# First batch's second and last third: one operation for all three feature blocks

## The chip, the cores and the metric

The kernel runs on one core of one Trainium2 chip. The metric is the device time of one execution in microseconds (us), 441.68 in the median of three runs (441.19 to 444.34). The engines are named as in the profile: PE does matmuls (PEld loads their weights), DVE, ACT and POOL do elementwise work, SP issues the DMA transfers. Each engine works through its own queue in order.

## The reference, cut to what matters

For 4 batches, 768 positions and 384 features (8 heads of 48), a linear attention with a complex decay runs first, and its output y is the input of a mixture of 4 attention experts:

```
mag = sqrt(a_re^2 + a_im^2); scale = min(mag, 0.999) / (mag + 1e-6)
S[t] = (a[t] * scale) * S[t-1] + k[t] v[t]^T   (complex, per feature d)
y[t] = q[t] . Re S[t]
for each expert e: q, k, v = x @ wq[e], wk[e], wv[e]
  a = causal softmax(q k^T / 8);  ye = a @ v @ wo[e]
out = sum over the two experts with the highest gate logits of w * ye
```

## The kernel before, in words

Features lie on the 128 partitions in three feature blocks j = 0, 1, 2 (384 = 3 x 128), positions in the free dimension. The recurrence is done in chunks of 128 positions: `logs` and `angles` turn the decay into running sums of log magnitude and angle by scans, and q and k are multiplied by exp, sin and cos of them (`logs`, `sincos`, `products`). For one j this takes about a dozen ACT activations in two table sets (logarithm and exponential, sine and arctangent), three scans per third on DVE or one long one, and a dozen products and other two-operand operations on DVE or POOL. The real and imaginary parts of q and k then lie in tile `qk`; `regroup` sends them by DMA to tile `fm`, where a head's 96 rows stand together: ten transfers (DMA issues on SP) for one third of a batch, three, four and three of them for j = 0, 1, 2.

From `fm`, PE works on pairs of chunks: transposes (`pk`), scores (`psc`, masked by DVE into `pts`), states (`pu`; `wst` and `tst` on DVE or POOL), outputs (`yu`, split by ACT and DVE into the tile `x`), then the expert projections (`proj`: `pp`, `qka`; `vproj`: `pv`), row maxima (`maxpass`: `pm`, DVE) and, once all six chunks are through, `rowmax` (`mrow`), `score` (`pss`, exponentials `pe` on ACT), `av` (`po`), `norm` (`dn`, `r`, `ot`) and `wo` (`pw`, `ob`, the output transfer).

Batches 1 to 3 take a whole feature block of 768 positions in one operation. Batch 0 is worked out in three thirds of 256 positions, so that its first third reaches PE early: the loop over `c` and `j` in `record` calls each step for one third and one feature block.

What runs when is written out by hand in tables. ORDER lists all operations, and since each engine runs its own in that order, the list sets every queue. HOME moves an operation to another engine than its own. ROOMS gives each tile its buffer. FILL names operations of PE ahead of which so many fill matmuls are issued: 128x512 products of the constant `keep` into a result buffer that the operation overwrites.

Of the kernel before, what the change touches and what calls it, by code (L numbers as in the profile page):

```python
# [40 lines left out]
HOME = {39: 'vector',  # L41
 54: 'vector',
 62: 'vector',
 69: 'vector',
# [108 lines left out]
 1420: 'gpsimd',
 1426: 'gpsimd',
 1428: 'gpsimd',
 1448: 'gpsimd',
 1450: 'gpsimd',
 1455: 'gpsimd',
 1463: 'gpsimd',
# [31 lines left out]
 1775: 'vector',
 1782: 'vector',
 1784: 'vector',
 1836: 'gpsimd',
 1858: 'gpsimd',
 1860: 'gpsimd',
 1868: 'gpsimd',
 1876: 'gpsimd',
 1929: 'vector',
 1935: 'vector'}  # L200

FILL = {297: 138, 358: 14, 376: 1, 407: 3, 460: 15, 466: 4, 509: 3, 737: 6}

ROOMS = {'ab': [0, 1, 0, 1, 0, 1, 0, 1, 0, 0, 1, 0],
 'carry': [0, 1, 0, 3, 1, 2],
 'fm': [0, 1, 0, 0, 1, 0, 1, 0, 1, 0, 1, 0],
 'gcf': [0, 0, 0, 0],
 'gmx': [0, 0, 0, 0],
# [744 lines left out]
```

## Time and profile before

| | |
|---|---|
| median of three runs | 441.68 us |
| profiled execution | 442.14 us, of which the span is 440.1 us |
| PE busy | 409.8 us (93%), fill matmuls among it |
| DVE busy | 367.6 us (84%), 758 instructions |
| ACT busy | 290.2 us (66%), 485 instructions, 37 table loads of 1.28 us among them |
| POOL busy | 149.9 us (34%), 153 instructions |
| granted clock of PE | 0.996 over the span |

The span runs from the first to the last instruction. Busy time of PE holds the fill matmuls too, so its share does not tell how much of the span is the program's own work. Of the other engines the share is an average over stages: in the first 120 us they are nearly full, in the last 140 us they are not.

### The profile page before, as it was taken

How to read it: one execution, taken by the hardware profiler on the slowest of the kernel's cores; microseconds unless marked ns; L12 is line 12 of the kernel's file. 1: busy time of each engine (PE TensorE's matmuls, PEld its weight loads, DVE VectorE, ACT ScalarE, POOL GpSimd, SP SyncE). 2: the span in 40 equal slices, each digit the busy share in tenths (PEclk: the TensorE clock that was granted, in tenths of full speed). 3: DMA queues.
4: the chain of work that ended last, by engine and by line, in shares of the span. 5: the costliest groups of instructions: out<-in, count | busy, mean ns of one | idle time of the engine just before them, and what ended most of it. 6: DMA issues, size and time to landing. Idle time of an engine off the chain costs nothing.

```text
span 440.1 us, 9745 instructions
## 1 busy us (share of the span) xinstructions
PE 409.8 (93%) x3804; PEld 329.3 (75%) x3804; DVE 367.6 (84%) x758; ACT 290.2 (66%) x485; POOL 149.9 (34%) x153
## 2 busy tenths in 40 slices
PE   7998897878899998997999989999999999999996
PEld 3447686856568886886879878788888988888675
DVE  6999989989977999999886899999876436798563
ACT  6999979788852899875644899777733313113562
POOL 0005212414340333494723533562625032200620
PEclk9999999899999999999999999999999999999999
DMA  8752759352463851303873810353371600101002
GB/s 268 284 160 57 194 178 318 97 180 68 103 193 82 229 186 36 104 2 87 255 208 101 247 65 2 110 162 108 103 194 35 176 3 18 55 20 37 19 1 107
DMA packets 28173, 53.40 MB, mean 121 GB/s; under 512 B 3552, under 2 KB 8928, under 8 KB 28128
## 3 DMA queue, kind: packets, MB, share of 16 engines
q1 hardware_dynamic: 28128, 52.79, 41.0%
q8 instruction: 30, 0.49, 0.5%
q14 instruction: 15, 0.12, 0.1%
HBM read 26.74 MB, written 4.72 MB: 71 GB/s over the span
## 4 chain that ended last, share of the span: by engine, by line
PE 51%; DVE 21%; ACT 17%; issue 5%; DMA 3%; POOL 2%; SPq 1%; DVEq 0%; ACTq 0%; POOLq 0%
DVE qk L897 9%; PE pss L897 8%; PE pp L897 7%; PE po L897 6%; ACT qk L897 5%; PE yu L897 5%; PE psc L897 5%; PE pw L897 5%; ACT ab L897 5%; ACT L895 4%; PE pu L897 3%; PE pv L897 3%; DVE ab L897 3%; DVE junk L897 3%; PE dn L897 2%
## 5 line engine op out<-in xcount | busy, mean ns | idle before, releaser
L897 ACT ACTIVATE pe<-pss 128x1024 f32<-128x1024 f32 (+2 forms) x48 | 43.3, 916 | 23.3 <-PE pss L897 19.7
L897 PE MATMUL psc<-fm 96*128 96x128 f32 x384 | 53.0, 285 | 5.2 <-DVE pts L897 2.1
L897 POOL TENSOR_TENSOR pe<-pe 128x512 f32<-128x512 f32 (+2 forms) x31 | 39.4, 1272 | 47.8 <-DVE pe L897 23.9
L897 PEld LDWEIGHTS psc<-fm 96*128 96x128 f32 x384 | 47.1, 194 | 9.8 <-DVE pts L897 2.4
L897 ACT ACTIVATE ab<-ab 128x768 f32<-128x768 f32 (+1 forms) x72 | 45.8, 654 | 8.7 <-DVE ab L897 7.3
L897 ACT ACTIVATE qk<-qk 128x256 f32<-128x256 f32 (+3 forms) x84 | 45.6, 563 | 7.4 <-DVE qk L897 5.7
L897 POOL TENSOR_TENSOR qk<-qk,ab 128x768 f32<-128x768 f32 (+1 forms) x25 | 39.0, 1568 | 28.6 <-ACT ab L897 16.0
L895 ACT ACT_TABLE_LOAD x37 | 47.5, 1283 | 1.4 <-PEq L942 0.8
L897 PE MATMUL pp<-x,whi 128*128 128x256 f32 x288 | 47.2, 287 | 0.5 <-DVE pts L897 0.3
L897 PE MATMUL pss<-qka 64*128 64x256 f32 (+3 forms) x480 | 46.4, 304 | 1.1 <-ACT pe L897 1.1
L897 PE MATMUL po<-pe,v 128*64 128x256 f32 (+3 forms) x320 | 43.5, 395 | 0.0
L897 POOL TENSOR_TENSOR qk<-qk 128x768 f32<-128x768 f32 (+1 forms) x18 | 25.1, 1406 | 53.8 <-ACT qk L897 47.7
L897 PEld LDWEIGHTS pss<-qka 64*128 64x128 f32 x480 | 35.5, 185 | 10.4 <-issue 4.2
L897 PEld LDWEIGHTS pp<-x,whi 128*128 128x128 f32 x288 | 38.9, 188 | 3.6 <-issue 1.1
L897 POOL TENSOR_SCALAR_AFFINE_SELECT pe<-pe 128x256 f32<-128x256 f32 x48 | 22.0, 474 | 53.0 <-ACT pe L897 52.9
L897 DVE TENSOR_TENSOR pts<-psc,keep 128x512 f32<-128x512 f32 x48 | 32.5, 683 | 9.1 <-PE yu L897 4.8
L886 PEld LDWEIGHTS <-keep 128*128 128x128 bf16 x184 | 18.1, 101 | 24.9 <-issue 3.0
L886 PE MATMUL psc<-keep 128*128 128x512 bf16 x144 | 33.6, 397 | 2.6 <-DVE keep L897 2.6
L897 DVE CUSTOM_DVE_ANT_0 junk<-pm,negm 128x128 bf16<-128x128 f32 (+3 forms) x64 | 31.0, 485 | 2.0 <-PE pm L897 0.3
L897 PE MATMUL pw<-whi,ot 128*128 128x384 f32 x96 | 28.6, 351 | 3.4 <-DVE qka L897 2.5
L897 DVE TENSOR_TENSOR qk<-qk,ab 128x256 f32<-128x256 f32 (+1 forms) x47 | 30.9, 688 | 0.9 <-ACT qk L897 0.3
L897 PE MATMUL yu<-pts,vt 128*64 128x128 f32 x384 | 27.7, 283 | 4.0 <-DVE pts L897 4.0
(118 smaller groups left out, 907.7 us busy)
## 6 DMA issues: line engine op xcount, KB each, us to landing
fm<-qk SPq DMA_DIRECT2D x72, 192.8 KB, 3.7
qk<-in_ak_dram SPq DMA_DIRECT2D x12, 768.0 KB, 6.9
ab<-in_ak_dram SPq DMA_DIRECT2D x18, 384.0 KB, 4.5
...
```

What stands on the lines that cost most here:

```text
L886: nc.tensor.matmul(z, real(plan.busy), real(plan.busy)[:, None, :].to_broadcast([128, 4, 128]), start=True, stop=True)
L895: nc.scalar.preload_act_table_set(need)
L897: getattr(getattr(nc, engine), name)(*a, **k)
```

## The change: batch 0's thirds 1 and 2 for all feature blocks at once

In batch 0 the first third is still worked out feature block by feature block. For the second and the last third each step is now called once for the three blocks: operations on 128x256 become operations on 128x3x256. The scans over positions stay 256 long. For this the twelve tiles `qk` (one per batch and feature block, in three rooms) become one tile with a place for each feature block, which all batches use, and the three decay tiles of a third become one with the part before the feature block. ORDER, HOME, FILL and ROOMS are new throughout. ACT now has 435 instructions in its queue and had 487, DVE 727 and had 760, POOL 145 and had 158, SP 224 as before; PE has the same matmuls in a new order, with 164 fill matmuls where there were 184 (135 ahead of the first real one, where there were 138). The number of table loads is the same.

The diff without the tables ORDER, HOME and ROOMS (rows of their effect stand below it):

```diff
-FILL = {297: 138, 358: 14, 376: 1, 407: 3, 460: 15, 466: 4, 509: 3, 737: 6}
+FILL = {199: 3, 205: 1, 211: 135, 217: 3, 227: 11, 262: 3, 370: 7, 405: 1}
...
@@ -407,7 +387,9 @@
     def cst(shape, dtype, name):
         return p.tile(shape, dtype, name)
 
-    ab, early, qk, fm, vt, xk, qka, v2, lgs, mrow, mx, ot = ({} for _ in range(12))
+    ab, early, fm, vt, xk, qka, v2, lgs, mrow, mx, ot = ({} for _ in range(11))
+
+    qk = p.tile([128, 3, 2, NK, KW], F32, "qk")
 
     def load_decay(b, j, k0, k1, split):
         n = (k1 - k0) * C2
@@ -415,8 +397,8 @@
             t = ab[b, j, k0] = p.tile([128, 2, n], F32, "ab")
         else:
             if k0 not in early:
-                early[k0] = p.tile([128, 3, 2, n], F32, "ab")
-            t = ab[b, j, k0] = early[k0][:, j]
+                early[k0] = p.tile([128, 2, 3, n], F32, "ab")
+            t = early[k0][:, :, j]
         x = ak[b, j, :, :2 * S].rearrange("p (x c) -> p x c", x=2)[:, :, k0 * C2:k1 * C2]
         for i in range(2):
             if split:
@@ -425,9 +407,7 @@
                 p.dma(t, x)
 
     def load_qk(b, j, k0, k1):
-        if (b, j) not in qk:
-            qk[b, j] = p.tile([128, 2, NK, KW], F32, "qk")
-        p.dma(qk[b, j][:, 0, k0:k1, :2 * C2], ak[b, j, :, 2 * S:].rearrange("p (k x) -> p k x", k=NK)[:, k0:k1])
+        p.dma(qk[:, j, 0, k0:k1, :2 * C2], ak[b, j, :, 2 * S:].rearrange("p (k x) -> p k x", k=NK)[:, k0:k1])
 
     def load_v(b, k):
         vt[b, k] = p.tile([128, 2, H, HD], F32, "vt")
@@ -487,69 +467,84 @@
             p.copy(whi[:, s], t)
             p.tt(V, wlo[:, s], t, mid(whi[:, s]), OP.subtract)
 
-    def views(b, j, k0, k1):
-        t, u = ab[b, j, k0], qk[b, j]
-        A, Bi = (t[:, i] for i in range(2))
-        flat = [x.rearrange("p (k x) -> p k x", x=C2) for x in (A, Bi)]
-        Q, K, X, Y = (u[:, i, k0:k1, o:o + C2] for i in range(2) for o in (0, C2))
-        return A, Bi, *flat, Q, K, X, Y, u[:, :, k0:k1, 2 * C2:]
-
-    def logs(b, j, k0, k1):
-        A, Bi, Af, Bf, Q, K, X, Y, E = views(b, j, k0, k1)
-        p.act(X, Af, AF.Ln)
-        p.act(Af, X, AF.Exp, scale=-1.0)
+    def views(b, js, k0, k1):
+        if b:
+            j = js[0]
+            t = ab[b, j, k0].rearrange("p i (k x) -> p i k x", x=C2)
+            Q, K, X, Y = (qk[:, j, i, k0:k1, o:o + C2] for i in range(2) for o in (0, C2))
+        else:
+            s = slice(js[0], js[-1] + 1)
+            t = early[k0][:, :, s]
+            Q, K, X, Y = (qk[:, s, i, k0, o:o + C2] for i in range(2) for o in (0, C2))
+        return t[:, 0], t[:, 1], Q, K, X, Y
+
+    def logs(b, js, k0, k1):
+        A, Bi, Q, K, X, Y = views(b, js, k0, k1)
+        n = NK if b else len(js)
+        p.act(X, A, AF.Ln)
+        p.act(A, X, AF.Exp, scale=-1.0)
         p.mul(V, Bi, Bi, A)
         p.act(A, Bi, AF.Square)
-        p.act(Y, Af, AF.Ln, bias=1.0)
+        p.act(Y, A, AF.Ln, bias=1.0)
         p.stt(X, Y, 0.5, X, OP.mult, OP.add)
         p.act(Y, X, AF.Exp, scale=-1.0)
         p.act(Y, Y, AF.Ln, scale=1e-6, bias=1.0)
         p.stt(X, X, math.log(0.999), Y, OP.min, OP.subtract)
-        for k in range(k1 - k0):
+        for k in range(n):
             p.put(V, "tensor_tensor_scan", X[:, k], cmask, X[:, k], 0.0, op0=OP.mult, op1=OP.add)
         p.act(Y, X, AF.Exp)
-        p.copy(E.rearrange("p x k c -> p k x c"),
-               Y.rearrange("p k (c t) -> p k c t", t=C)[:, :, None, :, C - 1].to_broadcast([128, k1 - k0, 2, 2]))
+        ends = Y.rearrange("p k (c t) -> p k c t", t=C)[:, :, None, :, C - 1].to_broadcast([128, n, 2, 2])
+        if b:
+            p.copy(qk[:, js[0], :, k0:k1, 2 * C2:].rearrange("p x k c -> p k x c"), ends)
+        else:
+            p.copy(qk[:, js[0]:js[-1] + 1, :, k0, 2 * C2:], ends)
         p.mul(V, Q, Q, Y)
         p.act(X, X, AF.Exp, scale=-1.0)
         p.mul(V, K, K, X)
 
-    def atan(b, j, k0, k1):
-        A, Bi = views(b, j, k0, k1)[:2]
+    def atan(b, js, k0, k1):
+        Bi = views(b, js, k0, k1)[1]
         p.act(Bi, Bi, AF.Arctan)
 
-    def angles(b, j, k0, k1):
-        A, Bi, Af, Bf, Q, K, X, Y, E = views(b, j, k0, k1)
+    def angles(b, js, k0, k1):
+        A, Bi = views(b, js, k0, k1)[:2]
         n = (k1 - k0) * C2
-        p.put(V, "tensor_tensor_scan", A, ones.to_broadcast([128, n]), Bi, last.get((b, j), 0.0), op0=OP.mult, op1=OP.add)
-        if k1 < NK:
-            last[b, j] = p.tile([128, 1], F32, "carry")
-            p.put(V, "tensor_copy", last[b, j], A[:, n - 1:n])
+        if b:
+            flat = [x.rearrange("p k x -> p (k x)") for x in (A, Bi)]
+            p.put(V, "tensor_tensor_scan", flat[0], ones.to_broadcast([128, n]), flat[1], 0.0, op0=OP.mult, op1=OP.add)
+        else:
+            for i, j in enumerate(js):
+                p.put(V, "tensor_tensor_scan", A[:, i], ones.to_broadcast([128, n]), Bi[:, i], last.get(j, 0.0), op0=OP.mult, op1=OP.add)
+            if k1 < NK:
+                c = p.tile([128, 3], F32, "carry")[:, :len(js)]
+                p.put(V, "tensor_copy", c, A[:, :, n - 1])
+                for i, j in enumerate(js):
+                    last[j] = c[:, i:i + 1]
         p.act(Bi, A, AF.Copy, scale=0.5 / math.pi, bias=MAGIC)
-        whole = Bi.bitcast(I16).rearrange("p (n w) -> p n w", w=2)[:, :, 0]
+        whole = Bi.bitcast(I16).rearrange("p k (n w) -> p k n w", w=2)[:, :, :, 0]
         p.stt(A, A, 0.5 / math.pi, whole, OP.mult, OP.subtract)
         p.act(Bi, A, AF.Abs)
 
     last = {}
 
-    def sincos(b, j, k0, k1):
-        A, Bi = views(b, j, k0, k1)[:2]
+    def sincos(b, js, k0, k1):
+        A, Bi = views(b, js, k0, k1)[:2]
         p.act(A, A, AF.Sin, scale=TWO_PI)
         p.act(Bi, Bi, AF.Sin, scale=-TWO_PI, bias=halfpi)
 
-    def products(b, j, k0, k1):
-        A, Bi, Af, Bf, Q, K, X, Y, E = views(b, j, k0, k1)
-        p.mul(V, X, Q, Af)
-        p.mul(V, Y, K, Af)
-        p.mul(V, Q, Q, Bf)
-        p.mul(V, K, K, Bf)
+    def products(b, js, k0, k1):
+        A, Bi, Q, K, X, Y = views(b, js, k0, k1)
+        p.mul(V, X, Q, A)
+        p.mul(V, Y, K, A)
+        p.mul(V, Q, Q, Bi)
+        p.mul(V, K, K, Bi)
 
     def regroup(b, k, js=(0, 1, 2)):
         if (b, k) not in fm:
             fm[b, k] = p.tile([96, H, KW], F32, "fm")
         for h, d, j, r, n in pieces():
             if j in js:
-                p.dma(fm[b, k][2 * d:2 * d + 2 * n, h], qk[b, j][r:r + n, :, k])
+                p.dma(fm[b, k][2 * d:2 * d + 2 * n, h], qk[r:r + n, j, :, k])
 
     kt, pt, st = {}, {}, {}
 
@@ -795,19 +790,19 @@
         if b == 0:
             ws = weights()
             weights_split(ws)
-            for c in range(NK):
+            for c, groups in enumerate((((0,), (1,), (2,)), ((0, 1, 2),), ((0, 1, 2),))):
                 for j in range(3):
                     load_decay(0, j, c, c + 1, False)
                     if c == 0:
                         load_qk(0, j, 0, NK)
                 for f in (logs, atan, angles, sincos, products):
-                    for j in range(3):
-                        f(0, j, c, c + 1)
+                    for js in groups:
+                        f(0, js, c, c + 1)
         for j in range(3 if b else 0):
             load_qk(b, j, 0, NK)
             load_decay(b, j, 0, NK, True)
             for f in (logs, atan, angles, sincos, products):
-                f(b, j, 0, NK)
+                f(b, (j,), 0, NK)
         for c in range(NC):
             if c % 2 == 0:
                 load_v(b, c // 2)
```

Place 1, POOL, its first operations on data (batch 0's thirds 1 and 2, then batch 1; `tst` belongs to the state of batch 0). Before:

```order
L897 TENSOR_SCALAR ab<-ab 128x256
L897 TENSOR_TENSOR ab<-ab 128x256
L897 TENSOR_TENSOR qk<-qk,ab 128x256 x3
L897 TENSOR_TENSOR qk<-qk 128x256
L897 TENSOR_TENSOR qk<-qk,ab 128x256 x2
L897 TENSOR_TENSOR qk<-qk 128x256 x3
L897 MEMSET mx_708 128x128
L897 TENSOR_TENSOR qk<-qk 128x256
L897 TENSOR_TENSOR qk<-qk,ab 128x256 x2
L897 TENSOR_TENSOR tst<-wst_836,fm 96x384
L897 TENSOR_TENSOR qk<-qk 128x3x256 x2
```

and with the change:

```order
L892 MEMSET mx_70 128x128
L892 TENSOR_TENSOR qk<-qk,ab 128x3x256
L892 TENSOR_TENSOR tst<-wst_733,fm 96x384
L892 TENSOR_TENSOR tst<-wst_766,fm 96x384
L892 MEMSET mx_775 128x128
L892 TENSOR_TENSOR qk<-qk 128x3x256 x2
L892 TENSOR_TENSOR ab<-ab 128x768
L892 TENSOR_TENSOR qk<-qk,ab 128x3x256
```

Of batch 0's products and other small operations, fourteen on 128x256 were POOL's; one on 128x3x256 is left to it, the others are on DVE and ACT.

Place 2, DVE, the last products of batch 0's last third. Before:

```order
L897 TENSOR_TENSOR qk<-qk,ab 128x256 x4
L897 SCALAR_TENSOR_TENSOR ab<-col,carry,ab 128x256
L897 TENSOR_TENSOR pts<-psc,keep 128x512
L897 SCALAR_TENSOR_TENSOR ab<-ab 128x256
L897 TENSOR_TENSOR qk<-qk 128x256 x2
L897 TENSOR_SCALAR ab<-ab 128x256
L897 TENSOR_TENSOR qk<-qk,ab 128x256
L897 TENSOR_TENSOR qka<-pp,qka 128x2x256
L897 TENSOR_TENSOR qk<-qk,ab 128x256
L897 CAST qka<-pp 128x2x256
L897 TENSOR_TENSOR qk<-qk,ab 128x256
L897 TENSOR_TENSOR qka<-pp,qka 128x2x256
```

and with the change:

```order
L892 TENSOR_TENSOR qk<-qk 128x3x256
L892 SCALAR_TENSOR_TENSOR ab<-ab 128x768
L892 COPY qk<-qk 128x6x2
L892 TENSOR_SCALAR ab<-ab 128x768
L892 TENSOR_TENSOR qk<-qk 128x3x256
L892 TENSOR_TENSOR wst_565<-pu,tst 96x384
L892 TENSOR_TENSOR qk<-qk,ab 128x3x256 x2
L892 TENSOR_TENSOR tst<-wst_565,fm 96x384
L892 TENSOR_TENSOR qk<-qk,ab 128x3x256 x2
L892 TENSOR_TENSOR wlo<-wst,whi 128x1028
L892 TENSOR_TENSOR pts<-psc,keep 128x512 x2
```

The pieces of one third were spread among other work, and stand together now; what they hand to `regroup` is complete only with the last of them.

Place 3, PE, the end of the program, from the last `cb` (behind the last `dn`) to the first matmul of the last output group (`ot_5079` before, `ot_5015` now). Before:

```order
L897 MATMUL cb<-cft,pick 64x128
L897 MATMUL pw<-whi,ot_4999 128x384
L897 MATMUL pw<-wlo,ot_4999 128x384
L897 MATMUL pw<-whi,ot_4999 128x384 x2
L897 MATMUL pw<-wlo,ot_4999 128x384
L897 MATMUL pw<-whi,ot_4999 128x384 x2
L897 MATMUL pw<-wlo,ot_4999 128x384
L897 MATMUL pw<-whi,ot_4999 128x384 x2
L897 MATMUL pw<-wlo,ot_4999 128x384
L897 MATMUL pw<-whi,ot_4999 128x384
L897 MATMUL pw<-whi,ot_5079 128x384
```

and with the change:

```order
L892 MATMUL cb<-cft,pick 64x128
L892 MATMUL po<-pe,v_4456 64x256 x2
L892 MATMUL po<-pe,v_4512 64x256 x2
L892 MATMUL po<-pe,v_4512 64x128 x2
L892 MATMUL pw<-whi,ot_4863 128x384
L892 MATMUL pw<-wlo,ot_4863 128x384
L892 MATMUL pw<-whi,ot_4863 128x384 x2
L892 MATMUL pw<-wlo,ot_4863 128x384
L892 MATMUL pw<-whi,ot_4863 128x384
L892 MATMUL pw<-whi,ot_5015 128x384
```

The `po` group that stood ahead of the last `dn` stands behind it, and six `pw` matmuls of the older group follow where there were twelve. The last `ot` subtraction was on DVE and is on POOL.

## Rows read from the trace of the kernel before

**Rows 1.** Windows: us, busy us of each engine, granted clock, DMA share, GB/s.

```profile
34.50:53.50 19.00, 16.18 (x155) 13.08 (x154) 18.86 (x36) 18.13 (x42) 7.98 (x11) 1.00 0.45 110
53.50:121.00 67.50, 56.47 (x484) 46.54 (x482) 63.22 (x122) 55.24 (x82) 19.70 (x15) 0.97 0.54 159
121.00:300.00 179.00, 169.50 (x1718) 143.06 (x1717) 160.13 (x291) 128.57 (x192) 81.11 (x71) 1.00 0.46 132
300.00:420.00 120.00, 119.62 (x1176) 99.91 (x1174) 84.77 (x203) 48.61 (x82) 37.23 (x45) 1.00 0.23 64
```

**Rows 2.** Page, part 5: the weight loads of all fill matmuls.

```profile
L886 PEld LDWEIGHTS <-keep 128*128 128x128 bf16 x184 | 18.1, 101 | 24.9 <-issue 3.0
```

**Rows 3.** Timeline of PE: start us, us, operation; opening fills, last fills, first score.

```profile
2.57 32.10 PE L886 MATMUL psc<-keep 128*128 128x512 bf16 x138 [2.57 <-DVE keep L897]
...
120.39 0.82 PE L886 MATMUL pss<-keep 128*128 128x512 bf16 x3
121.15 0.79 PE L897 MATMUL pss<-qka 64*128 64x384 f32 x6
```

**Rows 4.** Timeline of DVE up to 62 us: unhindered products, first and last stretched one.

```profile
21.99 3.44 DVE L897 TENSOR_TENSOR qk<-qk,ab 128x256 f32<-128x256 f32 x10 [0.31 <-ACT ab L897]
...
32.85 0.95 DVE L897 TENSOR_TENSOR qk<-qk 128x256 f32<-128x256 f32 x1
...
61.66 0.60 DVE L897 TENSOR_TENSOR qk<-qk,ab 128x256 f32<-128x256 f32 x1
```

**Rows 5.** Timeline of DVE, 62 to 121 us.

```profile
64.94 0.96 DVE L897 TENSOR_TENSOR ab<-ab 128x768 f32<-128x768 f32 x1 [1.29 <-ACT ab L897]
...
71.42 1.85 DVE L897 TENSOR_TENSOR_SCAN qk<-cmask,qk 128x256 f32<-128x256 uint8 x3
...
82.96 1.82 DVE L897 TENSOR_TENSOR qk<-qk,ab 128x768 f32<-128x768 f32 x2
...
89.89 0.69 DVE L897 TENSOR_TENSOR pts<-psc,keep 128x512 f32<-128x512 f32 x1 [1.50 <-PE psc L897]
...
92.72 3.45 DVE L897 TENSOR_TENSOR_SCAN qk<-cmask,qk 128x256 f32<-128x256 uint8 x3
```

**Rows 6.** Timeline of POOL: the operations beside the stretched ones.

```profile
32.72 0.81 POOL L897 TENSOR_TENSOR ab<-ab 128x256 f32<-128x256 f32 x1 [16.28 <-ACT ab L897]
...
93.44 2.18 POOL L897 TENSOR_TENSOR ab<-ab 128x768 f32<-128x768 f32 x1 [5.87 <-ACT ab L897]
```

**Rows 7.** POOL's groups by shape: count, busy us, mean ns, idle before.

```profile
L897 POOL TENSOR_TENSOR qk<-qk,ab 128x256 f32<-128x256 f32 x7 | 6.0, 863 | 12.7 <-ACT ab L897 6.9 <-DVE ab L897 5.4 <-DVE qk L897 0.4
L897 POOL TENSOR_TENSOR ot<-r,ot 128x256 fp32r<-128x256 f32 x5 | 4.4, 880 | 23.7 <-ACT ot L897 23.7
L897 POOL TENSOR_TENSOR qk<-qk 128x256 f32<-128x256 f32 x5 | 3.6, 722 | 6.1 <-ACT qk L897 6.1
```

**Rows 8.** DVE's groups by shape.

```profile
L897 DVE COPY kts<-pk 128x384 f32<-128x384 f32 x8 | 4.3, 549 | 0.7 <-PE pk L897 0.7
L897 DVE TENSOR_TENSOR ot<-r,ot 128x256 fp32r<-128x256 f32 x3 | 1.3, 421 | 0.0
```

**Rows 9.** Timeline of ACT: four small operations and two large ones back to back.

```profile
13.39 1.33 ACT L897 ACTIVATE ab<-ab 128x256 f32<-128x256 f32 x4
...
99.64 1.58 ACT L897 ACTIVATE ab<-ab 128x768 f32<-128x768 f32 x2 [1.48 <-DVE ab L897]
```

**Rows 10.** Timeline of PE: the end of the program.

```profile
430.65 0.65 PE L897 MATMUL dn<-pe,oner 128*64 128x256 f32 x4
...
433.37 0.34 PE L897 MATMUL pw<-whi,ot 128*128 128x384 f32 x1
434.29 0.44 PE L897 MATMUL pw<-whi,ot 128*128 128x384 f32 x1 [0.58 <-ACT ob L897]
```

**Rows 11.** SP's queue: six regroup transfers issued.

```profile
27.88 4.47 SPq L897 DMA_DIRECT2D fm<-qk  x6
```

**Rows 12.** Windows: the stretch with the lowest granted clock.

```profile
80.00:86.00 6.00, 4.92 (x40) 4.70 (x42) 5.96 (x15) 5.12 (x8) 1.73 (x1) 0.72 0.31 112
```

More of the change, by code (lines that the diff above doesn't have):

```diff
@@ L153 @@
[L153 to L159, printed above, removed]
+ 234: 'vector',
+ 237: 'vector',
+ 261: 'vector',
+ 270: 'gpsimd',
+ 274: 'vector',
+ 277: 'vector',
+ 286: 'gpsimd',
+ 305: 'vector',
+ 330: 'vector',
+ 332: 'vector',
+ 364: 'vector',
+ 416: 'gpsimd',
+ 418: 'gpsimd',
+ 423: 'gpsimd',
+ 431: 'gpsimd',
+ 450: 'gpsimd',
+ 470: 'gpsimd',
+ 477: 'gpsimd',
+ 485: 'gpsimd',
+ 496: 'gpsimd',
+ 502: 'gpsimd',
+ 514: 'vector',
@@ new lines @@
+ 526: 'vector',
+ 548: 'gpsimd',
+ 550: 'gpsimd',
+ 559: 'gpsimd',
+ 567: 'gpsimd',
+ 579: 'gpsimd',
+ 581: 'gpsimd',
+ 590: 'gpsimd',
+ 598: 'gpsimd',
+ 610: 'gpsimd',
+ 612: 'gpsimd',
+ 620: 'gpsimd',
+ 621: 'gpsimd',
+ 636: 'vector',
+ 659: 'gpsimd',
+ 668: 'vector',
+ 674: 'vector',
+ 675: 'vector',
+ 678: 'vector',
+ 714: 'vector',
+ 717: 'vector',
+ 744: 'vector',
+ 804: 'vector',
+ 807: 'vector',
+ 856: 'gpsimd',
+ 863: 'gpsimd',
+ 870: 'vector',
+ 871: 'gpsimd',
+ 882: 'gpsimd',
+ 898: 'gpsimd',
@@ new lines @@
+ 912: 'gpsimd',
+ 936: 'gpsimd',
+ 942: 'gpsimd',
+ 952: 'gpsimd',
+ 988: 'gpsimd',
+ 990: 'gpsimd',
+ 993: 'vector',
+ 1001: 'gpsimd',
+ 1019: 'gpsimd',
+ 1021: 'gpsimd',
+ 1029: 'gpsimd',
+ 1031: 'gpsimd',
+ 1032: 'gpsimd',
+ 1049: 'gpsimd',
+ 1050: 'gpsimd',
+ 1052: 'gpsimd',
+ 1060: 'gpsimd',
+ 1061: 'gpsimd',
+ 1062: 'gpsimd',
+ 1063: 'gpsimd',
+ 1076: 'vector',
+ 1087: 'vector',
+ 1090: 'vector',
+ 1099: 'gpsimd',
+ 1114: 'vector',
+ 1115: 'vector',
+ 1141: 'vector',
+ 1143: 'vector',
+ 1154: 'vector',
@@ L160 @@
+ 1166: 'gpsimd',
+ 1232: 'vector',
+ 1244: 'vector',
+ 1296: 'gpsimd',
+ 1298: 'gpsimd',
+ 1311: 'gpsimd',
+ 1320: 'gpsimd',
+ 1328: 'gpsimd',
+ 1337: 'vector',
+ 1357: 'gpsimd',
+ 1364: 'vector',
+ 1365: 'gpsimd',
+ 1370: 'gpsimd',
+ 1376: 'gpsimd',
+ 1382: 'gpsimd',
+ 1384: 'gpsimd',
+ 1417: 'vector',
+ 1427: 'gpsimd',
+ 1430: 'gpsimd',
+ 1440: 'gpsimd',
+ 1458: 'vector',
+ 1459: 'gpsimd',
+ 1461: 'gpsimd',
+ 1469: 'gpsimd',
+ 1471: 'gpsimd',
  1472: 'gpsimd',
- 1480: 'gpsimd',
  1490: 'gpsimd',
+ 1492: 'gpsimd',
@@ L191 @@
[L191 to L200, printed above, removed]
[L202 to L206 removed]
+ 1500: 'gpsimd',
+ 1501: 'gpsimd',
+ 1502: 'gpsimd',
+ 1503: 'gpsimd',
+ 1530: 'vector',
+ 1539: 'gpsimd',
+ 1554: 'vector',
@@ L207 @@
+ 1555: 'vector',
+ 1557: 'vector',
+ 1594: 'vector',
+ 1597: 'vector',
+ 1606: 'gpsimd',
+ 1610: 'vector',
+ 1615: 'vector',
+ 1622: 'vector',
+ 1659: 'gpsimd',
+ 1663: 'vector',
+ 1736: 'gpsimd',
+ 1760: 'gpsimd',
+ 1770: 'gpsimd',
+ 1804: 'vector',
+ 1831: 'vector',
+ 1832: 'gpsimd'}
+FILL = {199: 3, 205: 1, 211: 135, 217: 3, 227: 11, 262: 3, 370: 7, 405: 1}
+ROOMS = {'ab': [1, 0, 1, 0, 1, 0, 0, 1, 0, 1, 0, 1],
+ 'carry': [0, 1, 3, 0],
+ 'fm': [0, 1, 0, 0, 1, 0, 0, 1, 0, 0, 1, 0],
  'gcf': [0, 0, 0, 0],
```

150 lines of the change are left out of this document (14 added, 136 removed), and 166 rows, old and new, of tables (ORDER, ROOMS).

## The prediction

> **What bounds the kernel now.** I read the windows by stage first [rows 1], since the shares over the whole span mix stages. From 300 us on PE is busy 119.6 of 120 us: there only matmuls removed from its queue, or waits, count. In front of that DVE is the full engine: 18.86 of 19.0 us between 34.5 and 53.5 us and 63.22 of 67.5 us up to 121 us, while PE has 56.47 of 67.5 us with fill matmuls counted in. So I read the timeline of PE for these fills next: 138 of them in 32.10 us, one each 0.233 us, end at 34.7 us, where the first real work begins; the last three end just ahead of the first `score` at 121.15 us [rows 3]. The 184 weight loads of fills [rows 2] say that all of PE's 42.9 us of filling lies ahead of that matmul. The first 121 us are thus a stage in which PE waits for batch 0's features, and the change is made in that stage. The rest, 121 to 300 us, has PE busy 169.5 of 179 us: 9.5 us of waits, to be gained or lost by another order.
>
> **The change part by part.** The sum is made against the profiled execution, 442.14 us, which lies 0.46 us above the median of 441.68; the differences are applied to the median.
>
> Nothing is changed in what PE computes. The 20 fills that go (3 at the start, 0.7 us; 17 net later) give nothing by themselves: a fill stands where PE would have waited. They show what the new order expects to fill, not what comes.
>
> *DVE ahead of the first `score`.* Counted in the two queues up to the first `mrow`, on which `score` rests: 51 operations of 256 go. Ten of them back to back take 3.44 us with the last one whole [rows 4], so one each 0.335 us: -17.1 us. Five scalings on 256 and two small copies go; they have no row of their own, and at half to all of such a product they are 1.2 to 2.3 us; I take -1.2. Nineteen operations of 768 come: two back to back take 1.82 us, 0.96 for one alone [rows 5], so 0.86 each: +16.4. Three more evictions net come at 0.549 us, the row of `kts` [rows 8]: +1.6. Together **-0.3 us**. Merging saves DVE only 0.14 us for every three operations (3 x 0.335 against 0.86), and most of that pays for what POOL hands over (place 2 of the order and place 1).
>
> *What POOL's small operations cost DVE.* They are removed, and I think this is the larger half. DVE's first product at 32.85 us took 0.95 us, where such a one takes 0.41 (3.44 less nine steps) [rows 4]; beside it POOL worked from 32.72 us on, 0.81 us [rows 6]. Between that row and the one at 61.66 us (0.60 us) ten entries of the timeline are stretched like this, by 3.7 us in all, all beside one of POOL's twelve `qk` operations on 256 (6.0 and 3.6 us [rows 7]) or of two on `ab`. With the change one operation of 768 is left there, and two more of that size come ahead of the first `score`. Between 62 and 121 us ten of that size ran on POOL, and the dearest meeting is that at 93.44 us: three scans took 3.45 instead of 1.85 us [rows 5, 6]. Spread over ten that is 0.2 us each. So **-3.7 + 0.6 = -3.1 us**; the ends are 0 (the gain is eaten by waits for ACT) and, for the three that come, 1.6 us each.
>
> The Trainium skill, page "SBUF — State Buffer", section "SBUF: two separate sides", says that DVE with two operands and POOL hold their common port in turn, for a whole instruction. By that rule all 9.6 us of POOL's twelve could come back to DVE, not 3.7. The trace agrees that DVE stands still beside POOL, but not that it does so each time.
>
> *ACT.* Four small activations back to back take 1.33 us and two large ones 1.58 [rows 9]: 0.31 and 0.75 us a step, so 0.17 us saved per triple, and some 22 triples: 3.8 us. ACT had 55.2 of 67.5 us of work there [rows 1]; DVE's load covers it, so I cost it at nothing. If DVE's cover goes, the wait of 1.29 us for ACT at 64.94 us and that of 1.50 us for PE at 89.89 [rows 5] are next.
>
> *Regroup transfers on SP.* A third's ten transfers now wait for the last product of all three feature blocks. Six issues took 4.47 us, 0.745 each [rows 11]. Where formerly the last feature block's three were issued behind the last product, ten are: seven more, 5.2 us. Against it the merged products of third 1 stand earlier in DVE's queue. SP is idle most of the stage, and PE begins on four heads as they land. I take 0; the ends are a gain of nothing and a loss of 5.2 us per third (a rival below).
>
> *Between 121 and 420 us.* DVE has three operations of 768 fewer there (-2.6 us), POOL two more that can meet DVE (+0.4). DVE is busy 160 of 179 us, PE's waits are 9.5 us [rows 1]. I let half of 2.2 us arrive: **-1.1 us**. The order is new everywhere, so I bound this by a third of PE's waits either way, 3.2 us.
>
> *The end* (place 3). The last `dn` ends at 431.30 us, and PE resumes with the last output group at 434.29: a chain of 2.99 us, covered by twelve `pw` matmuls and `cb` up to 433.71, which leaves 0.58 us [rows 10]. The last subtraction moves from DVE (0.421 us) to POOL (0.880) [rows 7, 8]: 3.45 us. The cover becomes six `pw` (half of 2.4) and six `po` (I take 0.6): 1.8. The wait grows to 1.65 us, by **+1.1 us**; ends 0 and 1.6.
>
> The sum: -0.3 - 3.1 - 1.1 + 1.1 = -3.4, so 438.7 us for an execution like the profiled one and **438.3 us** for the median. A measurement of this kernel can tell about 1% from no change, 4.4 us: the forecast lies inside.
>
> **The rivals.**
> *DVE and ACT both get ahead, and the planned gaps close.* All 23 fills that go between 53.5 and 121 us (31 before, 8 now) are then time gained, 5.3 us, with 0.7 at the start: -6.0 - 1.1 + 1.1 = -6.0, 435.7 us. For it: ACT loses 3.8 us, POOL most of its small work, and DVE's two waits of 1.29 and 1.50 us can go too. Against it: DVE at 94% of 67.5 us with only 3.4 us less to do. Chance 0.30.
>
> *POOL's small operations held DVE throughout.* All 9.6 us return: -0.3 - 9.6 + 0.6 = -9.3, 432.4 us. For it the rule above; against it the ten stretched entries of only 3.7 us. Chance 0.04.
>
> *The regroup of whole thirds makes PE wait.* If the ten transfers stand on the path at both thirds, 10.4 us come: 438.3 + 10.4 = 448.7 us, slower. It decides once more than 7.8 of the 10.4 us fall on PE, or 3.4 us to be slower than before at all. For it: place 2, where the last product ends all. Against it: third 1's products are done earlier. Chance 0.10.
>
> *PE's clock falls.* At 80 to 86 us PE was granted 0.72 of its clock, a mix of its levels 1.2 and 2.4 GHz [rows 12]: 28% of 6 us, 1.7 us. If the five places that lose their fills after 53.5 us each did this, 8.5 us come: 446.8 us. For it: these fills go in a stage where PE still waits. Against it: a PE that waits loses little by a slower clock. Chance 0.08. The Trainium skill, page "TensorE: Matmul & The Clock Gate", section "Part 1: The HAM clock gate", has the slow clock as the default that activity lifts; the dip is what the trace shows of that.
>
> That the change does not do what it says is excluded by the queues: 52 instructions fewer on ACT, 33 on DVE, 13 on POOL, table loads equal.
>
> **How the numbers follow.** Forecast within 1% (438.3 us): 0.48. Faster by over 1% (below 437.3): 0.30 + 0.04 = 0.34. Slower by over 1%: 0.10 + 0.08 = 0.18. The best bounds, -6.0 - 3.2 + 0, reach 432.5 us; the worst, -0.3 + 3.2 + 1.6, reach 446.2. I give 432.5 to 446, which leaves out most of the two slower rivals.
>
> **What would show it.** DVE's products ahead of 62 us at 0.41 us with few stretched ones; the first `score` about 3 us earlier, at 118; DVE's load in 53.5 to 121 us still over 90%; PE's wait ahead of the last output group near 1.6 us. It is wrong if the first `score` comes at 115 us or earlier, if PE waits for `fm` by several us at thirds 1 or 2, or if the granted clock shows new dips.

## The result: 424.37 us, 4.1% faster

The changed kernel takes 424.37 us in the median (424.13 to 426.43, four runs), the old one on the same chip 443.01 (441.19 to 444.75). The ratio is 0.959, 95% interval 0.9533 to 0.9647. The profiled spans are 422.8 and 440.1 us: 17.3 us went. The forecast had 3.4 us, and its range ended at 432.5.

### The profile after, by three stretches

Both programs work out `mrow` eight times on DVE. The two of batch 0 cut the span into three stretches in which PE has nearly the same work in both kernels: a front that ends with the first `mrow`, a seam up to the second, and the rest. The windows of the kernel before (us, busy us of PE, PEld, DVE, ACT, POOL with counts, granted clock, DMA share, GB/s):

```profile
0.00:120.11 120.11, 103.68 (x770) 73.55 (x770) 111.46 (x248) 103.23 (x197) 29.51 (x34) 0.99 0.58 173
120.11:143.36 23.25, 22.02 (x237) 17.11 (x239) 17.27 (x43) 10.40 (x17) 6.78 (x8) 1.00 0.51 140
143.36:440.10 296.74, 284.07 (x2803) 238.65 (x2801) 238.86 (x470) 176.62 (x273) 113.64 (x111) 1.00 0.34 99
```

and of the changed kernel:

```profile
0.00:112.41 112.41, 98.42 (x745) 70.25 (x745) 103.96 (x212) 100.01 (x147) 24.78 (x22) 0.98 0.59 175
112.41:134.78 22.37, 22.18 (x248) 18.05 (x247) 18.03 (x44) 10.29 (x17) 8.38 (x10) 1.00 0.71 191
134.78:422.80 288.02, 280.18 (x2795) 237.13 (x2793) 227.90 (x473) 174.95 (x270) 113.95 (x109) 1.00 0.35 102
```

The front is 7.7 us shorter, the seam 0.9, the rest 8.7. In the front DVE is the full engine in both, 111.46 of 120.11 and 103.96 of 112.41 us: its idle time is 8.7 and 8.5 us, so the 7.7 us are 7.5 us of DVE's work. In the rest, DVE has as many instructions as before (473 for 470) and is busy 11 us less; PE is idle there for 7.8 instead of 12.7 us. The other 3.9 us of the rest's gain are busy time of PE (284.07 and 280.18 us, with eight matmuls fewer in the stretch); no run here takes them apart.

Why DVE has less to do shows in its groups by shape. Some of the front before (count | busy us, mean ns | idle before):

```profile
L897 DVE TENSOR_TENSOR_SCAN qk<-cmask,qk 128x256 f32<-128x256 uint8 x18 | 13.6, 786 | 0.1
...
L897 DVE SCALAR_TENSOR_TENSOR qk<-qk 128x256 f32<-128x256 f32 x18 | 8.3, 479 | 1.2 <-ACT qk L897 1.0
...
L897 DVE TENSOR_TENSOR qk<-qk 128x256 f32<-128x256 f32 x13 | 6.2, 498 | 0.0
...
L897 DVE TENSOR_TENSOR tst<-wst,fm 96x384 f32<-96x384 f32 x2 | 2.5, 1225 | 0.0
```

and after:

```profile
L892 DVE TENSOR_TENSOR_SCAN qk<-cmask,qk 128x256 f32<-128x256 uint8 x18 | 11.4, 674 | 0.1
...
L892 DVE SCALAR_TENSOR_TENSOR qk<-qk 128x256 f32<-128x256 f32 x6 | 2.4, 420 | 0.7 <-ACT qk L892 0.7
...
L892 DVE TENSOR_TENSOR qk<-qk 128x256 f32<-128x256 f32 x6 | 2.3, 418 | 0.0
...
L892 DVE TENSOR_TENSOR tst<-wst,fm 96x384 f32<-96x384 f32 x2 | 1.1, 549 | 0.0
```

Read the means: the same operation takes 786 and 674 ns, 479 and 420, 498 and 418, 1225 and 549. An operation that takes longer than the same shape does elsewhere is called stretched here. These four groups and the products and scalings with `ab` (439 and 454 ns, now 420) were stretched by 6.3 us in all, the old counts times the differences of the means. The rest of the program shows the same, before:

```profile
L897 DVE TENSOR_TENSOR qk<-qk,ab 128x768 f32<-128x768 f32 x10 | 11.8, 1200 | 0.2 <-issue 0.2
...
L897 DVE SCALAR_TENSOR_TENSOR ab<-ab 128x768 f32<-128x768 f32 x6 | 7.3, 1219 | 0.2 <-ACT ab L897 0.2
...
L897 DVE TENSOR_TENSOR tst<-wst,fm 96x384 f32<-96x384 f32 x9 | 6.6, 733 | 0.3
L897 DVE TENSOR_TENSOR qk<-qk 128x768 f32<-128x768 f32 x4 | 6.1, 1520 | 0.3 <-ACT qk L897 0.3
```

and after:

```profile
L892 DVE TENSOR_TENSOR qk<-qk,ab 128x768 f32<-128x768 f32 x8 | 7.4, 951 | 0.8 <-issue 0.6 <-ACT ab L892 0.2
...
L892 DVE SCALAR_TENSOR_TENSOR ab<-ab 128x768 f32<-128x768 f32 x6 | 5.7, 948 | 0.0
...
L892 DVE TENSOR_TENSOR tst<-wst,fm 96x384 f32<-96x384 f32 x6 | 3.3, 546 | 0.1
...
L892 DVE TENSOR_TENSOR qk<-qk 128x768 f32<-128x768 f32 x1 | 0.9, 932 | 0.0
```

Here 1200 became 951 ns, 1219 became 948, 733 became 546, 1520 became 932: by the old counts 8.1 of DVE's 11 us.

What stretches them: laying POOL's timeline over DVE's, I summed how long POOL works beside a DVE operation (`tensor_tensor`, `scalar_tensor_tensor` or scan) whose operands all lie in SBUF, that is, none in a tile that PE writes. Such time is called a meeting below. Before it is 13.8 us up to the second `mrow` and 33.2 behind it; after, 5.0 and 24.2. POOL works about as long as before (149.9 and 147.1 us), but more of it beside evictions, where one operand is in PSUM. The changed kernel's POOL and DVE around 92 us:

```profile
90.45 1.82 POOL L892 TENSOR_TENSOR ab<-ab 128x768 f32<-128x768 f32 x1 [8.00 <-ACT ab L892]
...
90.98 1.28 DVE L892 TENSOR_TENSOR x<-yu,x 128x512 fp32r<-128x512 f32 x2
92.18 0.94 DVE L892 SCALAR_TENSOR_TENSOR ab<-ab 128x768 f32<-128x768 f32 x1
92.22 3.85 POOL L892 TENSOR_TENSOR qk<-qk 128x768 f32<-128x768 f32 x2
...
93.52 1.28 DVE L892 TENSOR_TENSOR qka<-pp,qka 128x512 fp32r<-128x512 f32 x2
```

DVE's two `x<-yu,x` and two `qka<-pp,qka` take 1.28 us a pair, as they do alone, with POOL at work all the time; DVE's 0.94 us on SBUF at 92.18 is not stretched either: here POOL was held, and its two took 3.85 us, where two such took 3.06 in the kernel before:

```profile
116.77 3.06 POOL L897 TENSOR_TENSOR qk<-qk 128x768 f32<-128x768 f32 x2 [8.81 <-ACT qk L897]
```

The Trainium skill, page "SBUF — State Buffer", section "SBUF: two separate sides", has this: the pair of ports that DVE and GpSimd share is an exclusive lock, which a DVE operation with two SBUF inputs or a GpSimd operation, whichever starts first, holds for the whole instruction. The rows above agree: DVE came first by 0.04 us and POOL's two took 0.79 us longer, and DVE's operations with an input in PSUM were not held.

The rows that answer to those shown ahead of the prediction: PE's opening fills and first `score`,

```profile
2.36 30.78 PE L881 MATMUL pk<-keep 128*128 128x512 bf16 x135 [2.36 <-DVE keep L892]
32.98 0.49 PE L892 MATMUL pk<-ident,fm 96*128 96x96 f32 x4
...
113.72 0.80 PE L892 MATMUL pss<-qka 64*128 64x384 f32 x6
```

the regroup of third 1 on SP,

```profile
37.76 6.91 SPq L892 DMA_DIRECT2D fm<-qk  x10
```

and the end of PE:

```profile
413.31 0.65 PE L892 MATMUL dn<-pe,oner 128*64 128x256 f32 x4
...
416.07 0.33 PE L892 MATMUL pw<-whi,ot 128*128 128x384 f32 x1
416.98 0.44 PE L892 MATMUL pw<-whi,ot 128*128 128x384 f32 x1 [0.58 <-ACT ob L892]
```

The first `score` came at 113.72 us; it was at 121.15 [rows 3] and was forecast for 118. Ten transfers of a third now go in one row of 6.91 us [rows 11], and PE does not wait for `fm`. The wait ahead of the last output group is 0.58 us as before [rows 10]. The clock's dip of 80 to 86 us [rows 12] stands at 92 to 100 us now, 0.79; there is no other ahead of the last microsecond.

### The profile page after: what moved, and what is told of

Read it like the earlier page. It is cut to its first block, busy times and chain, and to the rows that moved or that the text cites. A ratio compares the mean times of both kernels' runs of the same rounds, so it can differ in the third digit from the quotient of the medians.

```text
span 422.8 us, 9613 instructions
## 1 busy us (share of the span) xinstructions
PE 400.8 (95%) x3784; PEld 325.4 (77%) x3784; DVE 349.9 (83%) x725; ACT 285.3 (67%) x433; POOL 147.1 (35%) x140
## 4 chain that ended last, share of the span: by engine, by line
PE 59%; ACT 16%; DVE 12%; DMA 6%; SPq 3%; issue 3%; DVEq 0%; ACTq 0%
PE pss L892 9%; PE pp L892 8%; PE po L892 7%; PE pw L892 6%; PE psc L892 6%; ACT ab L892 6%; PE yu L892 5%; ACT qk L892 5%; DVE qk L892 5%; PE pv L892 4%; PE pu L892 4%; ACT L890 3%; PE pm L892 3%; DMA fm<-qk 3%; SPq L892 3%
## 5 line engine op out<-in xcount | busy, mean ns | idle before, releaser
L892 POOL TENSOR_TENSOR qk<-qk,ab 128x768 f32<-128x768 f32 x21 | 39.3, 1888 | 51.5 <-DMA ab<-in_ak_dram 34.2
L892 PE MATMUL psc<-fm 96*128 96x128 f32 x384 | 51.6, 280 | 0.9 <-DVE x L892 0.5
L892 ACT ACTIVATE qk<-qk 128x768 f32<-128x768 f32 (+2 forms) x63 | 42.5, 689 | 4.3 <-DVE qk L892 3.7
L892 POOL TENSOR_TENSOR pe<-pe 128x512 f32<-128x512 f32 (+2 forms) x26 | 36.7, 1410 | 22.0 <-DVE pe L892 16.9
L892 POOL TENSOR_TENSOR qk<-qk 128x768 f32<-128x768 f32 x17 | 29.7, 1758 | 26.6 <-ACT qk L892 10.4
L881 PE MATMUL pk<-keep 128*128 128x512 bf16 x138 | 31.6, 392 | 2.4 <-DVE keep L892 2.4
L881 PEld LDWEIGHTS <-keep 128*128 128x128 bf16 x164 | 16.3, 100 | 21.8 <-issue 2.5
L892 PEld LDWEIGHTS pu<-vt,kts 128*96 128x96 f32 x320 | 28.9, 165 | 4.4 <-ACT kts L892 2.5
L892 DVE TENSOR_TENSOR pe<-pe 128x512 f32<-128x512 f32 (+2 forms) x38 | 26.4, 694 | 6.8 <-PE po L892 3.1
L892 PE MATMUL pu<-vt,kts 128*96 128x48 f32 x320 | 30.2, 248 | 1.6 <-ACT kts L892 1.5
```

The costliest lines, as they stand in the source:

```text
L881: nc.tensor.matmul(z, real(plan.busy), real(plan.busy)[:, None, :].to_broadcast([128, 4, 128]), start=True, stop=True)
L892: getattr(getattr(nc, engine), name)(*a, **k)
```

## The experiments

The three stretches are cut at each trace's own `mrow` rows, as above. Where a kernel's ORDER is mixed of the two, an operation comes as early in its list as its inputs and a free buffer allow, and every tile has as many buffers as before.

### The tile alone, and the merge without the order

Run 1, one tile in the old kernel: the three feature blocks stay apart, all tables are the old ones.

```diff
-            for c, groups in enumerate((((0,), (1,), (2,)), ((0, 1, 2),), ((0, 1, 2),))):
+            for c, groups in enumerate((((0,), (1,), (2,)),) * NK):
```

> 

> The old order, homes and separate operations, with nothing of the change but the one tile for all q and k features (three operations of batch 3 stand up to nine places later, since one tile asks it). Rooms theory (the one tile lets loads and regroups start earlier and the new order is only how this is used): a large part of the gain comes, 435 us or less. Merge theory and order theory (the tile only allows the merge): no change, 441 to 444 us.

450.66 us, ratio 1.023 (1.018 to 1.028): neither theory, slower. One wait makes it, on ACT, and behind it on PE:

```profile
251.32 0.84 ACT L907 ACTIVATE qk<-ab 128x768 f32<-128x768 f32 x1 [7.97 <-DMA fm<-qk]
...
255.68 1.01 PE L907 MATMUL pp<-x,whi 128*128 128x256 f32 x3 [8.98 <-DVE pts L907]
```

Batch 3's first logarithm writes where batch 2's last regroup still reads, 8 us long; the old order had counted on another room. Without these 9.0 us the span of 448.8 is the old 440. The tile brings nothing by itself and costs where the order does not fit it.

Run 2, the changed order with the merge undone: each of 49 operations is issued as three.

```diff
-                    for js in groups:
-                        f(0, js, c, c + 1)
+                        for j in range(3):
+                            f(0, (j,), c, c + 1)
+                            three.append(p.ops[n:])
+                            del p.ops[n:]
+                        for x in zip(*three):
...
+                                p.ops.append([y[0] for y in x])
```

> 

> The changed kernel's order, homes, rooms and fills, with each of the 49 merged operations (the scans are three in both) issued as three on 256 columns at the same place. Merge theory (fewer and larger operations are the gain): 98 operations more cost DVE 0.14 us and ACT 0.17 us a triple, 3 to 4 us on each, and the first score goes back from 113.7 to 117 us or later; 428 to 434 us. Order theory (the new order, and what it no longer gives to GpSimd, is the gain): less than 2 us, 424 to 427 us.

426.62 us, 0.967 (0.963 to 0.972). Merging is worth about 2 us: 2.2 by the medians, 1.3 by the profiled spans (424.1 and 422.8), and the two intervals overlap. Its first `mrow` is at 114.52 us, 2.1 later than with the merge. The merge theory's 428 us or more did not come; the order theory holds.

Run 3, the old order with merged operations (ORDER is the old list with each triple at its last member's place):

> 

> The old order with the merged operations: each stands where the last of its three stood, on the engine that the changed kernel gives it, and everything else keeps its old order and engine. Merge theory: most of what came ahead of the first score comes here too, 430 to 437 us, first score at 117 us or earlier. Order theory: the merged operation waits for the last of its three, so nothing or a loss, 441 to 447 us.

475.26 us, 1.076 (1.069 to 1.084), worse than either theory had it; 9.2 us of it are run 1's wait. The first `mrow` comes at 142.66 us: each merged step waits for the last of three that the old order had staggered. PE's granted clock is 0.87 over this front, so some of the loss may be the clock's.

### Front and rest, apart

Runs 4 and 6, the new front and the old order behind it; run 6 sets the places of the feature blocks in the tile by a table `SLOT[b][j]`:

> 

> The changed kernel's order, homes and fills up to the first score (481 operations), then the old order and homes for all that is left. The first score should come at about 113.7 us, as in the changed kernel. Lead theory (what follows the first score follows from the front's lead, whatever the later order): 424 to 429 us. Later-order theory (the ten us behind the first score come from the new order of that stretch): the lead of 7.4 us is kept and no more, 434 to 437 us.

> 

> As the run with the new front and the old later order, but with the three feature blocks of the one tile in the places (per batch) that the old kernel's three tiles had, so that batch 3's first logarithm no longer waits for batch 2's regroup. The 7.6 us wait at 240 to 250 us should be gone. If the front's lead is kept by the old later order: 432 to 437 us. If it is lost at the seam: 440 to 444 us.

450.47 us (ratio 1.020) and 450.45 (1.021): neither says anything of the lead, since both have a wait of my own making. Run 4 has that of run 1, 7.6 us; in run 6 the places that I gave batch 1 made PE wait 7.7 us at 72 us, in the front. Run 4 showed one thing besides. Its front is the changed kernel's, but a first transfer landed 1.1 us later, PE's first real matmul came at 33.77 instead of 32.98 us, and PE's clock was at half from 44 to 48 us. The same `pu` matmuls, in the changed kernel and in run 4:

```profile
41.20 1.56 PE L892 MATMUL pu<-vt,kts 128*96 128x48 f32 x16 [0.66 <-ACT kts L892]
```

```profile
43.02 2.57 PE L887 MATMUL pu<-vt,kts 128*96 128x48 f32 x16 [1.00 <-ACT kts L887]
```

The first `mrow` came 3.8 us later than in the changed kernel (116.23); in run 10, with the same front and no such fall, 0.7.

Run 10 has places that fit both:

```diff
+SLOT = ((0, 1, 2), (0, 1, 2), (0, 2, 1), (2, 1, 0))
-        p.dma(qk[:, j, 0, k0:k1, :2 * C2], ...
+        p.dma(qk[:, SLOT[b][j], 0, k0:k1, :2 * C2], ...
```

> 

> New front, old later order, as twice before, with the places in the one tile taken so that batch 1 has those of the changed kernel, and batches 2 and 3 what the old three tiles gave them. Neither the 7.6 us wait at 250 us nor the 7.7 us wait at 72 us should come. The first mrow at 112 to 116 us and the old 320 us behind it: 433 to 438 us if the lead is kept; 440 us or more if the old later order loses it.

437.23 us, 0.988 (0.983 to 0.992). Run 5, the other way round, the old front and the new order behind it:

> 

> The old order, homes, fills and separate operations up to the first score, then the changed kernel's order and homes, with the one tile. The first mrow should come at about 120 us, as before. In the changed kernel 310.4 us follow the first mrow (422.8 less 112.4), in the old one 320.0 us (440.1 less 120.1). Later-order theory: the new later order is worth its 9.6 us by itself, 430 to 434 us. Lead theory (its gain comes only of what the new front has done ahead): 438 to 443 us.

436.14 us, 0.990 (0.987 to 0.993). The windows of run 10 and of run 5:

```profile
0.00:113.07 113.07, 100.45 (x745) 71.81 (x745) 103.95 (x212) 100.34 (x149) 26.04 (x22) 0.97 0.59 175
113.07:138.80 25.73, 24.29 (x242) 19.31 (x242) 16.53 (x43) 9.27 (x14) 6.89 (x9) 0.93 0.63 164
138.80:435.90 297.10, 284.11 (x2803) 238.70 (x2801) 238.67 (x470) 176.57 (x273) 113.69 (x111) 1.00 0.34 99
```

```profile
0.00:120.20 120.20, 103.43 (x770) 73.53 (x770) 111.58 (x248) 103.25 (x197) 29.66 (x34) 0.99 0.58 173
120.20:146.66 26.46, 23.46 (x243) 18.78 (x244) 19.46 (x42) 11.04 (x17) 10.59 (x10) 0.94 0.50 137
146.66:434.30 287.64, 279.71 (x2795) 236.90 (x2793) 229.13 (x473) 174.79 (x270) 115.97 (x109) 1.00 0.35 101
```

Read the last rows: with the old order the rest takes 297.1 us, whatever the front (296.7 before); with the new one 287.6, whatever the front (288.0). The front's 7 us and the rest's 9 us are two gains that do not need each other. Each run loses some 3 us in the seam (26.5 and 25.7 for 23 us), where its two orders meet and the granted clock is 0.93 and 0.94.

### What makes the front shorter

Run 8, as run 2, with the 14 small operations back on POOL; run 9, the old kernel with these 14 on DVE.

```diff
+            if n in SMALL.get(i, ()):
+                engine, name, a, k = moved("gpsimd", name, a, k)
```

> 

> As the changed order with every merged operation issued as three, and beyond that the 14 small operations of batch 0 that the old kernel gave to GpSimd are on GpSimd again. Without the 14 it took 426.6 us. Prediction's term (they hold DVE by 3.7 us, and take 14 times 0.4 us off it): 425 to 429 us. If what GpSimd does to DVE is larger than the prediction had it: 430 us or more.

> 

> The old kernel with nothing changed but the engine of the 14 small operations of batch 0 (256 columns) that it gave to GpSimd: they run on VectorE, in their old places. DVE gets 14 times 0.41 us more to do, 5.8 us. The prediction's own term (they hold DVE by 3.7 us): 1 to 3 us slower, 441 to 444 us. Theory from the two runs with the merged operations issued as three (430.3 against 424.1 us of span): they cost more than they relieve, by 5 to 7 us, also in the old order; 433 to 436 us.

Run 8: 432.01 us, 0.981 (0.977 to 0.985), 5.4 us more than run 2. Run 9: 440.51, 0.996 (0.992 to 0.999). The second `mrow` (us) tells the front and the seam apart from the rest:

| | 14 on POOL | 14 on DVE |
|---|---|---|
| old order | 143.36 (before) | 143.81 (run 9) |
| new order, triples issued singly | 143.56 (run 8) | 136.88 (run 2) |

In these four only the new order with the 14 on DVE gains, 6.5 us; the merge adds 2.1 to make 134.78. Run 9's theory fell: in the old order the 14 are worth what they cost. Its DVE front, beside that of the kernel before above:

```profile
L884 DVE TENSOR_TENSOR_SCAN qk<-cmask,qk 128x256 f32<-128x256 uint8 x18 | 13.2, 761 | 0.1
...
L884 DVE TENSOR_TENSOR qk<-qk 128x256 f32<-128x256 f32 x18 | 7.2, 414 | 0.2 <-ACT qk L884 0.2
L884 DVE SCALAR_TENSOR_TENSOR qk<-qk 128x256 f32<-128x256 f32 x18 | 7.2, 417 | 1.0 <-ACT qk L884 0.9
...
L884 DVE TENSOR_TENSOR tst<-wst,fm 96x384 f32<-96x384 f32 x2 | 2.5, 1228 | 0.0
```

By the old counts times the differences of the means (the `ab` groups, now 415 and 408 ns, among them) 3.8 us of stretch went with the 14. DVE, busy 112.3 us up to its first `mrow` at 120.6, is busy 0.8 us more than before (111.5), so the 14 themselves cost it some 4.6. Its scans still take 761 ns and its `tst` 1228, beside POOL's large operations, which stayed where they were: against 674 and 549 in the changed kernel that is 2.9 us (the two readings add to 6.7 us, not 6.3, since some means are a little lower here than in the changed kernel). Run 8 shows a meeting at its dearest (DVE, POOL and, last, PE):

```profile
33.29 1.75 DVE L908 TENSOR_TENSOR qk<-qk 128x256 f32<-128x256 f32 x5
35.01 5.04 DVE L908 TENSOR_TENSOR qk<-qk,ab 128x256 f32<-128x256 f32 x7
...
32.62 2.92 POOL L908 TENSOR_TENSOR qk<-qk 128x256 f32<-128x256 f32 x1 [14.19 <-DMA ab<-in_ak_dram]
35.50 3.94 POOL L908 TENSOR_TENSOR qk<-qk,ab 128x256 f32<-128x256 f32 x5
...
39.98 1.27 DVE L908 TENSOR_TENSOR pts<-psc,keep 128x512 f32<-128x512 f32 x2
...
40.71 0.66 PE L908 MATMUL yu<-pts,vt 128*64 128x128 f32 x8 [2.54 <-DVE pts L908]
```

Seven products take 5.04 us; with POOL idle seven took 2.42 in the changed kernel, at 23.43 us. The two `pts` right behind them, out of PSUM, take 1.27 us, with POOL at work for 0.65 us of it. But DVE's own time is the smaller part of run 8's loss. Up to the first `mrow`, 6.7 us later than in run 2 (121.19 and 114.52), DVE is busy 1.3 us more (108.3 and 107.0) and idle 5.4 us more: PE waited 2.54 us for the late `pts`, its granted clock was 0.50 from 44 to 52 us, and DVE then waited for what PE and ACT had late. The mean granted clock is 0.972 to 0.980 in all four runs of run 8, 0.991 or 0.992 in run 2's, so the fall belongs to this kernel; how much the meeting would cost without it is not shown.

Run 14 moves the last POOL product of the front too:

> 

> The changed kernel with the one product of third 1 (768 columns, 2.13 us on GpSimd at 35.6 us) that it left to GpSimd on VectorE as well. Alone it should take DVE 0.86 us. If every meeting of the two engines in the front costs DVE time, at most that is lost: 424 to 425.3 us, or up to 1 us won. It was not seen to stretch any of DVE's operations, so I expect 424.8 us.

425.55 us, 0.962 (0.958 to 0.966), which can't be told from the changed kernel's 0.959; first `mrow` at 113.34, 0.9 us later in the one trace. A product on POOL that meets no such DVE operation costs nothing that shows: what counts is where they meet.

### What makes the rest shorter

Run 11, the new order with the old engines behind the first `score`, and run 12, the old order with the new engines (HOME alone is changed):

> 

> The changed kernel's order, with the old choice of engine for every operation behind the first score (106 operations change engine). If the order itself carries the 8.7 us that the stretch behind the second mrow (batch 0) gained, 424 to 428 us. If it is which engine gets what: 431 us or more.

> 

> The old kernel's order, with the changed kernel's choice of engine for every operation behind the first score. If which engine gets what carries the gain of the later stretch by itself: 431 to 436 us. If the order does, or both together: 438 us or more.

439.54 us, 0.993 (0.989 to 0.997), and 457.86, 1.037 (1.030 to 1.044; the front is 2.5 us longer there too, with PE's clock down at 70 to 82 us). The rest takes, from the second `mrow` on:

| us (of it meetings) | old engines | new engines |
|---|---|---|
| old order | 296.7 (33.2) | 307.8 (32.4) |
| new order | 301.9 (36.9) | 288.0 (24.2) |

Neither the order nor the engines gain by themselves in this stretch; each loses with the other's. Some of the stretched operations come back in run 11, DVE in its rest:

```profile
L891 DVE TENSOR_TENSOR_SCAN qk<-cmask,qk 128x256 f32<-128x256 uint8 x18 | 16.6, 960 | 0.1
...
L891 DVE TENSOR_TENSOR tst<-wst,fm 96x384 f32<-96x384 f32 x9 | 6.9, 768 | 0.1
...
L891 DVE TENSOR_TENSOR qk<-qk 128x768 f32<-128x768 f32 x4 | 5.0, 1247 | 0.0
```

The scans' 960 ns stand against 681 in the changed kernel; products and scalings with `ab` stay at 960 and 953 ns there. In seven of the sixteen traces the rest is 286.8 to 288.0 us, with 24.1 to 27.3 us of meetings; in the other nine it is 296.7 us or more, with 30.7 or more. These seven all have one order and one choice of engines behind the first `score`, so the meetings do not stand apart from what else that choice sets. Among the nine, more meetings do not go with more time: run 12 has 0.8 us less of them than the kernel before and takes 11 us longer, and DVE is busy 235.0 us in run 11's rest and 237.4 in run 12's, both less than the 238.9 before. So the meetings fit the gain, but that they are its cause is not shown: PE's waits follow from many buffers, and I have no kernel that changes the meetings alone.

### Fills and the clock

Run 7 leaves out all fills but the first 135, run 13 adds nine ahead of the first `pv` at 92.41 us.

```diff
-FILL = {199: 3, 205: 1, 211: 135, 217: 3, 227: 11, 262: 3, 370: 7, 405: 1}
+FILL = {211: 135}
```

```diff
-FILL = {199: 3, 205: 1, 211: 135, 217: 3, 227: 11, 262: 3, 370: 7, 405: 1}
+FILL = {199: 3, 205: 1, 211: 135, 217: 3, 227: 11, 262: 3, 300: 9, 370: 7, 405: 1}
```

> 

> The changed kernel without its 29 fills behind the first real matmul (the 135 at the start stay). Cover theory (a fill stands where PE would wait anyway, as the prediction had it): 423 to 426 us, the granted clock as before. Clock theory: without them PE's clock falls in the stretches of 33 to 55 and 95 to 112 us to 1.2 GHz, as it fell at 43 to 50 us in the run with the new front and the old later order, 3 us a time; 427 to 433 us.

> 

> The changed kernel with nine more fills, about 2 us, ahead of the first pv of batch 0's second third, where PE waits 2.06 us at 90.3 us and its granted clock is 0.77 to 0.81 for the next 8 us. If that slow stretch lies on the path: 1 to 2 us faster than the changed kernel's 424.4 us, 422.5 to 423.5 us. If PE waits for DVE there whatever its clock: no change, 424 to 425 us.

Run 7: 426.08 us, 0.966 (0.963 to 0.970); the granted clock is 0.72 from 48 to 60 us and 0.79 from 92 to 108, and the second `mrow` is 1.8 us later. If the fills are worth anything it is that, less than the clock theory's 3 us a time; the interval overlaps that of the changed kernel. Run 13: 426.98, 0.964 (0.961 to 0.967), not faster, and by its median slower, as neither theory had it, though here too the intervals overlap. Its first `mrow` comes at 114.80 us, 2.4 later:

```profile
92.26 2.92 PE L881 MATMUL pv<-keep 128*128 128x512 bf16 x9 [1.98 <-DVE x L892]
```

The fills waited 1.98 us for the same DVE operation that `pv` waits for, and then stood in front of it: `pv` began at 94.62 us, in the changed kernel at 92.41. They write `pv`'s bank, which held the `yu` that this operation reads. No version here beats the changed kernel.

## Why the prediction was wrong

**It read the stages rightly.** The front is DVE's, the sum over its two queues was the right working, and DVE's load from 53.5 us to the first `score` stayed over 90%. No wait for `fm` came, ACT's 3.2 us in the front (103.2 to 100.0) stayed covered, no new dip came. The rivals that end slower did not happen.

**The first step that failed is what POOL's operations cost DVE.** The sum had -3.1 us: 3.7 us of stretch that goes with the 14 small ones, 0.6 that comes with three large. For the 14 the size was right (3.8 us by run 9). The large ones had the wrong sign: their meetings, the scans of 3.45 us and the `tst` of 1225 ns among them, were spread over ten operations at 0.2 us each [rows 5, 6], and three more were priced the same. The new order ended these meetings instead, which gave back some 2.9 us. In all 6.3 us of stretch went where 3.1 were forecast, and DVE's work ahead of the first `mrow` fell by 7.5 us, not 3.4. The other 1.2 us stand, by subtraction, against the 0.3 that the count of operations had given. The first `score` at 113.72 us is earlier than 115, the mark that the prediction had set for being wrong.

**The larger failure is the step from 121 to 420 us.** It had -1.1 us, and the bound of 3.2 either way was a third of PE's waits. Measured it is -9, and it comes without the new front too (run 5). The bound looked at PE's waits only; DVE's own stretched operations, 1200 and 1520 ns where 0.96 us had been read [rows 5], stood in the same trace and were not priced. What the runs show in its place is that the later order and the later engines gain together and lose apart (runs 11 and 12); through which waits stays open. "Let half of 2.2 us arrive" priced three merged operations; what was changed there was the order and the engines of all that follows.

**The end** was priced at +1.1 us and came out at nothing. The chain from the last `dn` (ends 413.96) to the last group is 3.02 us, not 3.45, and `po` and `pw` cover 2.4 of it, not 1.8: twelve `po` stand there, 1.25 us, where I took six. The last subtraction, priced as a part of the chain, is not in it: the last group's first `pw` starts at 416.98 us while POOL's subtraction runs from 416.39 to 417.11, and in the kernel before it started at 434.29, with DVE's running from 433.95 to 434.38.

**The rivals.** "All gaps close" was near the front's size and wrong in its mechanism: DVE's idle time in the front stayed (8.7 and 8.5 us), its work shrank. "POOL held DVE throughout" was the nearest to the mechanism in the front, at a chance of 0.04; it took its size from how long POOL runs, where a meeting is dear by what DVE does in it. The Trainium skill's page "SBUF — State Buffer", section "SBUF: two separate sides", speaks of two SBUF inputs. The prediction wrote two operands, and so took it for a disagreement that some DVE operations beside POOL were not stretched; one of them was a `pts` out of PSUM, 0.68 us at 42.57 us in the kernel before, as it takes alone.
